# Splitting weights into high and low parts: the low parts move from VectorE to GpSimd in a kernel that schedules itself

## The chip, the cores and the metric

The kernel runs on one core of a Trainium2 chip. That core has a matrix engine (PE, with its weight loads shown apart as PEld), a vector engine (DVE), a scalar engine (ACT), GpSimd (POOL) and a queue engine that issues transfers (SP). The metric is the device time of one execution in microseconds; a kernel's figure is the median of its runs.

## The reference

```
sig = 1 / (1 + exp(-f_logit));  f = lb + (1 - lb) * sig          # (2, 6080, 256)
h[t] = f[t] * h[t-1] + (1 - f[t]) * x[t];  y[t] = h[t]           # scan along each sequence
a = relu(y.reshape(12160, 256) @ w_in)                           # w_in: 256 x 2048, float64
out = ((a * a) @ w_out).astype(float32)                          # w_out: 2048 x 256, float64
```

A gated scan over the tokens of two sequences, then a two-layer MLP with a squared ReLU. The weights arrive as float64, x and f_logit as float32.

## The kernel before

**Arithmetic.** PE multiplies in float32r, which keeps fewer bits than float32. So every operand v is split: `hi` is v rounded to float32r (made by ACT), `lo` is v - hi (made by DVE until now), and one product is three passes of PE: hi by hi, lo by hi and hi by lo. A few early products ("plain": `PLAIN_1`, `PLAIN_2`) use unsplit float32 operands, each costing PE four passes.

**Weights.** They come in as 64-bit integers and are turned into float32 on the chip, chunk by chunk, in `prepare_w`. For one chunk: DVE masks the exponent (`exponent`, L237), ACT rebiases it (`rebias`, L242), DVE sets sign and power (`power`, L270), DVE masks the mantissa, from a second copy loaded with a shift of some bytes (`mantissa_whole`, L257), or in two instructions (L248, L264), DVE multiplies both into the float32 weight (`whole`, L277), ACT rounds it to `w_h` (`high`, L292), and DVE subtracts to get `w_l` (`low`, L295). There are 15 chunks: two of 128 columns, three of 256, six of 512 and four of 1,024. The temporaries `e` and `w` are pools of two buffers, so a chunk's mantissa waits until the `high` and `low` of the chunk two before it have read theirs.

**Tokens.** The first 960 tokens are two blocks of 480 columns (`scan_x`): sigmoid (L352) and gate (L355) on ACT, a multiply (L361) and the scan (L368) on DVE, `high` (L384) on ACT, `low` on DVE: L388 for block 0, which also scales, and L393 for block 1, a plain subtraction. While these two blocks go through the MLP the weights are still being made. This stretch, up to the first product of pair 0 (the `bank_b` matmul), is called the ramp here. After it come 11 pairs of column blocks (up to 2 x 512), in a loop over 8 steps each, whose order is written out by hand and which the diff leaves alone.

**The scheduler.** In the ramp no order is written by hand. Each operation is a `Job` with an engine, a price in us and the jobs it comes after. `set_due` gives each a due time, counted back from the times at which PE is to need it (8.0 us plus 0.217 us for each pass). `emit_all` then plays the engines forward: at each step it takes the engine that can start soonest and, of the jobs ready there, the one due first. The order so found is the order in which each engine's instructions are written, so on the chip every engine runs them strictly in that order, each waiting for its inputs. Where the play leaves PE idle before 24 us, `idle` writes in matmuls on a dummy operand (`po<-t2h` in the trace) as filler.

The prices of the two engines concerned:

```python
def on_dve(n, emit, *after, rate=960):
    return Job("DVE", 0.075 + n / rate, emit, *after)

def on_act(n, emit, *after, base=0.1):
    return Job("ACT", base + n / 1200, emit, *after)
```

All transfers of the ramp are issued by SP. In the ramp's steady part POOL does nothing; its five instructions are memsets at the very start.

Of the kernel before, what the change touches and what calls it, by code (L numbers as in the profile page):

```python
# [7 lines left out]
F32 = mybir.dt.float32  # L8
# [8 lines left out]
ALU = mybir.AluOpType  # L17
# [6 lines left out]
def gated_scan_then_relu2_mlp(  # L24
# [13 lines left out]
    nc = tc.nc  # L38
# [18 lines left out]
    for row in range(T // seq):  # L57
        end = (row + 1) * seq
        while at < end:
            h = min(NB, (end - at) // 2)  # L60
# [32 lines left out]
    def pin(ins):  # L93
        return tc.keep_in_program_order(ins) if pinned[0] else ins


    class Job:

        def __init__(self, engine, cost, emit, *after, lag=None, load=0):
            self.engine, self.cost, self.emit, self.load = engine, cost, emit, load  # L100
            self.lag = cost + LAG[engine] if lag is None else lag
            self.after = [a for a in after if a is not None]
# [1 line left out]
            self.number = len(jobs)  # L104
            jobs.append(self)

    LAG = {"PE": 0.17, "DVE": 0.08, "ACT": 0.1, "SP": 0.0}
    SEEN = 0.04
    PASS = 0.217
    AWAIT = 0.02  # L110
# [15 lines left out]
    def on_dve(n, emit, *after, rate=960):  # L126
        return Job("DVE", 0.075 + n / rate, emit, *after)

    def on_act(n, emit, *after, base=0.1):
        return Job("ACT", base + n / 1200, emit, *after)  # L130

    def set_due():

        kids = {}
        for x in jobs:
            for y in x.after:
                kids.setdefault(id(y), []).append(x)
        done = set()

        def due(x):  # L140
            if x.number not in done:
                done.add(x.number)
                dues = [due(k) - SEEN for k in kids.get(id(x), [])] + ([x.due] if x.due else [])
                x.due = min(dues) - x.lag if dues else 1e9
            return x.due

        for x in reversed(jobs):
            due(x)

    def emit_all():  # L150

        free = {"PE": 1.2, "DVE": 1.2, "ACT": 2.0, "SP": 0.7}
        wire = 2.9
        left = {id(x): len(x.after) for x in jobs}
        kids = {}
        for x in jobs:
            for y in x.after:
                kids.setdefault(id(y), []).append(x)
        ready = {e: [] for e in LAG}

        def open_up(x):
            x.ready = max([y.end + SEEN for y in x.after] or [0.0])
            ready[x.engine].append(x)

        for x in jobs:
            if not x.after:
                open_up(x)
        while any(ready.values()):
            start, e = min(
                (max(free[e], min(x.ready for x in xs)), e) for e, xs in ready.items() if xs)  # L170
            x = min((x for x in ready[e] if x.ready <= start + AWAIT),
                    key=lambda x: x.number if e == "SP" else x.due)
            start = max(start, x.ready)
            if e == "PE":
                idle(start - free[e], start)
            ready[e].remove(x)
            pinned[0] = True
            x.emit()
            pinned[0] = False
            free[e] = start + x.cost  # L180
            x.end = start + x.lag
            if x.load:
                wire = max(start + 2.2, wire)
                wire = x.end = wire + x.load / (265e3 if wire < 6.3 else 375e3)
            for k in kids.get(id(x), []):
                left[id(k)] -= 1
                if not left[id(k)]:
                    open_up(k)
        assert all(x.end is not None for x in jobs)
# [32 lines left out]
    def prepare_w(m, a, n, load):  # L222
# [3 lines left out]
        hi, lo = w_h2[m // 2][:, a:a + n], w_l2[m // 2][:, a:a + n]  # L226
        tmp = {}
# [64 lines left out]
            pin(nc.scalar.activation(out=hi, in_=tmp["w"], func=AF.Copy))  # L292

        def low():
            pin(nc.vector.tensor_tensor(out=lo, in0=tmp["w"], in1=hi.bitcast(F32), op=ALU.subtract))  # L295

        old = sets[-2] if len(sets) > 1 else (None,) * 8
        e = on_dve(n, exponent, load, old[4], rate=1920)
# [11 lines left out]
        w = on_dve(n, whole, *f, s)  # L310
# [3 lines left out]
                k: on_act(P, lambda k=k: scaled(k), w, base=0.25)  # L314
                for k in range(b // P, min(b + n, D) // P)})
        h = on_act(n, high, w)
        l = on_dve(n, low, h)
        sets.append((e, i, f, s, w, h, l))
        raw_jobs.setdefault(m // 2, []).extend((e, s) if m in SHIFT else (e, *f, i, s))
        return h, l  # L320
# [7 lines left out]
    def operand(name, part):  # L328
        return xs.tile([P, NB], F32R, tag=f"{name}{part}", name=f"{name}{part}")
# [3 lines left out]
    def scan_x(j):  # L333

        t, n, first = blocks[j]
        f, x, g = {}, {}, {}

        def fetch(got, src, nm, k):
            def emit():
                if not got:  # L340
                    sb = fx.tile([P, KD, NB], F32, tag=f"{nm}{j}", name=f"{nm}in")
                    got.update({i: sb[:, i, :n] for i in range(KD)})
                    got["all"] = sb
                at = slice(k, k + 1)
                pin(nc.sync.dma_start(out=got["all"][:, at, :n], in_=src[:, at, t:t + n]))
            return emit

        def sig(k):
            if j == 0 and k == 0:
                o = io.tile([P, KD, NB], F32, tag="ob", name="gate")  # L350
                g.update({i: o[:, i, :n] for i in range(KD)})
            pin(nc.scalar.activation(out=f[k], in_=f[k], func=AF.Sigmoid))  # L352

        def lin(k):
            pin(nc.scalar.activation(  # L355
                out=g[k] if j == 0 else f[k], in_=f[k], func=AF.Identity,
                scale=olb_sb[:, k:k + 1], bias=lb_sb[:, k:k + 1],
            ))

        def mul(k):  # L360
            pin(nc.vector.scalar_tensor_tensor(  # L361
                out=x[k], in0=f[k], scalar=1.0, in1=x[k], op0=ALU.subtract, op1=ALU.mult,
            ))

        def run(k):
            i = n_scan[0] // KD % 2
            n_scan[0] += 1
            pin(nc.vector.tensor_tensor_scan(  # L368
                out=x[k], data0=g[k] if j == 0 else f[k], data1=x[k],
                initial=0.0 if first else st[k][1 - i], op0=ALU.mult, op1=ALU.subtract,  # L370
            ))
            x_in[j] = x

        def keep(k):

            scale = {"func": AF.Identity, "scale": olb_sb[:, k:k + 1]} if j == 0 else {"func": AF.Copy}
            pin(nc.scalar.activation(out=st[k][j], in_=x[k][:, n - 1:n], **scale))

        def high(k):
            if j not in x_h:  # L380
                x_h[j] = [operand(o, "h")[:, :n] for o in HOME[j]]
                x_l[j] = [operand(o, "l")[:, :n] for o in HOME[j]]
            scale = {"func": AF.Identity, "scale": olb_sb[:, k:k + 1]} if j == 0 else {"func": AF.Copy}
            pin(nc.scalar.activation(out=x_h[j][k], in_=x[k], **scale))  # L384

        def low(k):
            if j == 0:
                pin(nc.vector.scalar_tensor_tensor(  # L388
                    out=x_l[j][k], in0=x[k], scalar=olb_sb[:, k:k + 1],
                    in1=x_h[j][k].bitcast(F32), op0=ALU.mult, op1=ALU.subtract,  # L390
                ))
            else:
                pin(nc.vector.tensor_tensor(  # L393
                    out=x_l[j][k], in0=x[k], in1=x_h[j][k].bitcast(F32), op=ALU.subtract))

        def loads_of(ks):
            return {(nm, k): Job("SP", 0.45, fetch(got, src, nm, k),
                                 load=P * 4 * n)
                    for k in ks for nm, got, src in (("f", f, fT), ("x", x, xT))}

        def jobs_of(loads, kept):
            out = {}
            for k in range(KD):
                a = on_act(n, lambda k=k: sig(k), loads.get(("f", k), loads["f", 0]))
                if j == 0:
                    c = on_dve(n, lambda k=k: mul(k), a, loads.get(("x", k), loads["x", 0]))
                    b = on_act(n, lambda k=k: lin(k), a, base=0.27)
                else:
                    b = on_act(n, lambda k=k: lin(k), a, base=0.27)
                    c = on_dve(n, lambda k=k: mul(k), b, loads.get(("x", k), loads["x", 0]))  # L410
                d = on_dve(n, lambda k=k: run(k), c, b, kept[k], rate=480)
                h = on_act(n, lambda k=k: high(k), d, base=0.27 if j == 0 else 0.1)
                s = on_act(1, lambda k=k: keep(k), d)
                l = on_dve(n, lambda k=k: low(k), h)
                out[k] = h, l, s, d
            return out

        return loads_of, jobs_of
# [390 lines left out]
    for js, m in tiles:  # L809
        while pend and pend[0][0] < m - 2:  # L810
            second_job(*pend.pop(0))
        high, low = first_jobs(js, m)
# [10 lines left out]
    after = [x for y in x_jobs for k in range(KD) for x in y[k][:3]] + [in_of[6][0][0]]  # L823
# [13 lines left out]
    sig, lin, neg, run, sub, hi, lo = pair_steps(0)  # L837
# [26 lines left out]
    first, high, low = sums_w(0)  # L864
# [108 lines left out]
    for p, (_, h, _) in enumerate(pairs):  # L973
# [4 lines left out]
        for s in range(STEPS):  # L978
# [62 lines left out]
            if closing:  # L1041
                n = len(groups)
# [21 lines left out]
    n = len(groups)  # L1064
# [5 lines left out]
    at, h, _ = pairs[p]  # L1070
# [52 lines left out]
```

## Time and profile before

| | us |
|---|---|
| median of 3 runs (lowest to highest) | 997.66 (997.41 to 998.53) |
| the profiled execution, its own time | 996.66 |
| its span, first to last instruction | 994.7 |
| PE busy in the span | 989.3 |
| DVE busy | 748.7 |
| ACT busy | 721.6 |
| POOL busy | 0.7 |

The granted clock of TensorE is 1.00 over the whole execution. A matmul's duration in the trace is longer than the step to the next one, because matmuls overlap: it is the step, the difference of two starts, that says what one costs.

### The profile page before, as it was taken

The page shows a single profiled execution, that of the slowest core. Times are in us where ns is not written, and L with a number is a line of the kernel's source. Part 1 is how long each engine was busy: PE and PEld are TensorE (multiplying, and loading weights), DVE is VectorE, ACT ScalarE, POOL GpSimd, SP SyncE. Part 2 cuts the span into 40 slices and gives each one's busy share as a digit, 9 for nine tenths or more (in the row PEclk, how much of TensorE's full clock was granted, in tenths as well). Part 3 has the DMA queues.
Part 4 walks back from the last instruction along what each step waited for, and adds up shares of the span by engine and source line. Part 5 has one row for each costly group of instructions (what it writes and reads, how often), then busy time and mean ns, then how long its engine had stood idle before and what let it go on. Part 6 is the DMA issues. An engine that isn't in the chain of part 4 may idle for free.

```text
span 994.7 us, 11306 instructions
## 1 busy us (share of the span) xinstructions
PE 989.3 (99%) x4357; PEld 818.2 (82%) x4357; DVE 748.7 (75%) x929; ACT 721.6 (73%) x981; POOL 0.7 (0%) x5
## 2 busy tenths in 40 slices
PE   9999999999999999999999999999999999999998
PEld 5888888888888888888888888888888888888887
DVE  8997888687678677778767867867776876786555
ACT  8997988767677677776776767667677677676664
POOL 0000000000000000000000000000000000000000
PEclk9999999999999999999999999999999999999999
DMA  8942102102100200210210110021021021000001
GB/s 286 344 168 85 41 1 85 43 0 64 64 1 22 78 29 20 65 43 1 65 64 1 53 71 4 22 64 43 0 85 43 1 60 63 1 1 21 22 1 40
DMA packets 15893, 53.80 MB, mean 54 GB/s; under 512 B 1888, under 2 KB 4192, under 8 KB 15328
## 3 DMA queue, kind: packets, MB, share of 16 engines
q1 hardware_dynamic: 15552, 52.84, 15.4%
q8 instruction: 34, 0.56, 0.2%
q10 hardware_dynamic: 288, 0.25, 0.1%
q14 instruction: 19, 0.16, 0.1%
HBM read 40.63 MB, written 12.45 MB: 53 GB/s over the span
## 4 chain that ended last, share of the span: by engine, by line
PE 94%; DVE 3%; ACT 2%; DMA 1%; issue 0%; SPq 0%
PE po L434 68%; PE bank_b L434 24%; PE ph L434 2%; DMA shifted<-in_w_dram 1%; DMA fin<-in_f_logit_dram 0%; DVE e L270 0%; DVE gl L740 0%; DVE w_l L295 0%; DVE w L277 0%; DVE e L237 0%; DVE w L257 0%; DVE xin L368 0%; ACT e L242 0%; ACT w_h L292 0%; ACT fin L512 0%
## 5 line engine op out<-in xcount | busy, mean ns | idle before, releaser
L964 DVE TENSOR_TENSOR gl<-r,gh 128x1024 fp32r<-128x1024 f32 (+1 forms) x174 | 212.3, 1220 | 146.2 <-ACT r L933 89.7
L434 PE MATMUL po<-gh,w_h 128*128 128x512 f32 (+1 forms) x764 | 296.8, 388 | 0.0
L434 PE MATMUL po<-gh,w_l 128*128 128x512 f32 (+1 forms) x764 | 296.7, 388 | 0.0
L434 PE MATMUL po<-gl,w_h 128*128 128x512 f32 (+1 forms) x764 | 296.3, 388 | 0.0
L1037 ACT ACTIVATE r<-r 128x1024 f32<-128x1024 f32 (+1 forms) x87 | 92.1, 1058 | 131.5 <-DVE r L1031 131.5
L434 PEld LDWEIGHTS po<-gh,w_h 128*128 128x128 f32 x764 | 143.5, 188 | 30.8 <-ACT gh L730 0.6
L434 PEld LDWEIGHTS po<-gl,w_h 128*128 128x128 f32 x764 | 143.4, 188 | 29.1 <-DVE gl L964 0.5
L434 PEld LDWEIGHTS po<-gh,w_l 128*128 128x128 f32 x764 | 143.5, 188 | 28.1 <-issue 0.4
L942 ACT ACTIVATE gh<-r 128x1024 fp32r<-128x1024 f32 (+1 forms) x81 | 85.6, 1057 | 34.5 <-DVE r L937 34.5
L1031 DVE TENSOR_TENSOR r<-po,u 128x512 f32<-128x512 f32 (+1 forms) x88 | 60.6, 688 | 62.4 <-PE po L434 61.6
L1002 ACT ACTIVATE c<-bank_b 128x512 f32<-128x512 f32 (+1 forms) x88 | 52.5, 597 | 70.9 <-PE bank_b L434 70.9
L933 ACT ACTIVATE r<-r 128x1024 f32<-128x1024 f32 (+1 forms) x93 | 98.3, 1057 | 2.9
L929 ACT ACTIVATE gh<-r 128x1024 fp32r<-128x1024 f32 (+1 forms) x93 | 98.4, 1058 | 2.8
L937 DVE SCALAR_TENSOR_TENSOR r<-r 128x1024 f32<-128x1024 f32 (+1 forms) x81 | 98.2, 1213 | 0.0
L1024 DVE TENSOR_TENSOR r<-po,c 128x512 f32<-128x512 f32 (+1 forms) x88 | 60.6, 688 | 5.6 <-PE po L434 1.1
L1033 DVE TENSOR_TENSOR r<-bank_b,p 128x512 f32<-128x512 f32 (+1 forms) x88 | 60.6, 689 | 0.0
L1023 ACT ACTIVATE u<-bank_b 128x512 f32<-128x512 f32 (+1 forms) x88 | 52.5, 596 | 11.1 <-PE bank_b L434 1.9
L1017 ACT ACTIVATE p<-po 128x512 f32<-128x512 f32 (+1 forms) x88 | 50.8, 577 | 0.8 <-PE po L434 0.8
L1058 ACT ACTIVATE r<-bank_b 128x512 f32<-128x512 f32 (+1 forms) x87 | 50.2, 578 | 0.0
L532 DVE TENSOR_TENSOR_SCAN xin<-fin,small,xin 128x1024 f32<-128x1024 f32 (+1 forms) x20 | 46.6, 2331 | 0.0
L434 PE MATMUL po<-t1h,w_h 128*128 128x512 f32 (+1 forms) x88 | 34.3, 389 | 0.0
L434 PE MATMUL po<-t1h,w_l 128*128 128x512 f32 (+1 forms) x88 | 34.2, 389 | 0.0
(166 smaller groups left out, 1558.3 us busy)
## 6 DMA issues: line engine op xcount, KB each, us to landing
fin<-in_f_logit_dram SPq DMA_DIRECT2D x20, 512.0 KB, 4.2
xin<-in_x_dram SPq DMA_DIRECT2D x20, 512.0 KB, 3.6
out_dram<-ob SPq DMA_DIRECT2D x20, 512.0 KB, 2.6
shifted<-in_w_dram SPq DMA_DIRECT2D x14, 511.5 KB, 5.4
raw<-in_w_dram SPq DMA_DIRECT2D x4, 1024.0 KB, 6.9
raw<-in_w_dram SPq DMA_DIRECT2D x6, 512.0 KB, 5.9
out_dram<-ob SPq DMA_DIRECT2D x7, 240.0 KB, 2.0
fin<-in_f_logit_dram SPq DMA_DIRECT2D x4, 240.0 KB, 4.6
```

What stands on the lines that cost most here:

```text
L434: pin(nc.tensor.matmul(*args, **kw))
L929: pin(nc.scalar.activation(out=self.gh[:, :, :self.h], in_=self.r, func=AF.Square))
L933: pin(nc.scalar.activation(out=self.r, in_=self.r, func=AF.Square))
L937: pin(nc.vector.scalar_tensor_tensor(out=self.r, in0=self.r, scalar=0.0, in1=self.r, op0=ALU.max, op1=ALU.mult))
L942: pin(nc.scalar.activation(out=self.gh[:, :, :self.h], in_=self.r, func=AF.Copy))
L964: pin(nc.vector.tensor_tensor(out=self.gl[:, :, :self.h], in0=self.r, in1=self.gh[:, :, :self.h].bitcast(F32), op=ALU.subtract))
L1002: pin(nc.scalar.activation(out=c1, in_=B[:, :h], func=AF.Copy))
L1023: pin(nc.scalar.activation(out=u2, in_=B[:, :h], func=AF.Copy))
L1024: pin(nc.vector.tensor_tensor(out=r0[:, 0, :h], in0=Dk[:, :h], in1=c1, op=ALU.add))
L1031: pin(nc.vector.tensor_tensor(out=r0[:, 1, :h], in0=A[:, :h], in1=u2, op=ALU.add))
L1033: pin(nc.vector.tensor_tensor(out=r1[:, 1, :h], in0=B[:, :h], in1=p5, op=ALU.add))
L1037: pin(nc.scalar.activation(out=r0[:, :, :h], in_=r0[:, :, :h], func=AF.Relu))
```

## The change

The scheduler gets a fifth engine, POOL, with a price of 0.15 us plus one us for 460 columns, a lag of 0.15 us and a first free time of 2.0 us. Two kinds of jobs go there: `low` of all 15 weight chunks, and `low` of block 1's tokens (two instructions, one for each half of the model dimension). `low` of block 0, and the pairs' own `lo`, stay on DVE. Because prices and engine change, the scheduler may also find another order for every other instruction of the ramp.

```diff
-    LAG = {"PE": 0.17, "DVE": 0.08, "ACT": 0.1, "SP": 0.0}
+    LAG = {"PE": 0.17, "DVE": 0.08, "ACT": 0.1, "POOL": 0.15, "SP": 0.0}
...
+    def on_pool(n, emit, *after):
+        return Job("POOL", 0.15 + n / 460, emit, *after)
+
...
-        free = {"PE": 1.2, "DVE": 1.2, "ACT": 2.0, "SP": 0.7}
+        free = {"PE": 1.2, "DVE": 1.2, "ACT": 2.0, "POOL": 2.0, "SP": 0.7}
...
         def low():
-            pin(nc.vector.tensor_tensor(out=lo, in0=tmp["w"], in1=hi.bitcast(F32), op=ALU.subtract))
+            pin(nc.gpsimd.tensor_tensor(out=lo, in0=tmp["w"], in1=hi.bitcast(F32), op=ALU.subtract))
...
         h = on_act(n, high, w)
-        l = on_dve(n, low, h)
+        l = on_pool(n, low, h)
...
             else:
-                pin(nc.vector.tensor_tensor(
+                pin(nc.gpsimd.tensor_tensor(
                     out=x_l[j][k], in0=x[k], in1=x_h[j][k].bitcast(F32), op=ALU.subtract))
...
-                l = on_dve(n, lambda k=k: low(k), h)
+                l = (on_pool if j else on_dve)(n, lambda k=k: low(k), h)
```

## Rows read from the trace of the kernel before

**Rows 1.** The page's first part: busy us, share of the span, instructions of each engine.
```profile
PE 989.3 (99%) x4357; PEld 818.2 (82%) x4357; DVE 748.7 (75%) x929; ACT 721.6 (73%) x981; POOL 0.7 (0%) x5
```
**Rows 2.** Busy time by stretch; PE, PEld, DVE, ACT, POOL, clock, DMA share, GB/s.
```profile
9.05:20.15 11.10, 10.83 (x28) 4.80 (x27) 10.70 (x25) 11.10 (x26) 0.00 (x0) 1.00 0.79 297
20.15:90.70 70.55, 70.41 (x321) 59.59 (x320) 65.70 (x95) 65.14 (x99) 0.00 (x0) 1.00 0.65 232
...
5.00:59.40 54.40, 53.99 (x222) 40.79 (x221) 52.20 (x91) 53.12 (x94) 0.00 (x0) 1.00 0.88 323
```
**Rows 3.** Timeline of PE: start, us, instruction; start, one wait, end of the ramp.
```profile
1.31 7.90 PE L434 MATMUL po<-t2h 128*128 128x480 f32 x26 [1.31 <-POOL t2h L473]
9.05 3.38 PE L434 MATMUL ph<-xin,t4l 128*128 128x480 f32 x8
...
58.86 0.38 PE L434 MATMUL po<-gl,w_h 128*128 128x480 f32 x1
59.38 0.49 PE L434 MATMUL ph<-b11h,w_h 128*128 128x480 f32 x1
...
90.49 0.38 PE L434 MATMUL po<-gl,w_h 128*128 128x480 f32 x1
90.71 0.39 PE L434 MATMUL bank_b<-b11h,w_h 128*128 128x512 f32 x1
```
**Rows 4.** The start's gate and scan: timelines of ACT and DVE.
```profile
6.38 0.77 ACT L355 ACTIVATE gate<-fin,small 128x480 f32<-128x480 f32 x1
...
7.41 1.15 DVE L368 TENSOR_TENSOR_SCAN xin<-gate,xin 128x480 f32<-128x480 f32 x1
```
**Rows 5.** Chain of waits within the ramp: start, us, what; its stretches on DVE and DMA.
```profile
10.78 0.66 DVE xin L361
...
29.84 0.69 DVE e L270
...
37.58 7.30 DMA shifted<-in_w_dram
...
58.37 0.96 ACT w_h L292
```
**Rows 6.** Busy time of line 295 alone, by stretch: length, DVE busy, clock, DMA share.
```profile
5.00:20.00 15.00, 1.53 (x5) 1.00 0.84 307
20.00:30.00 10.00, 1.66 (x3) 1.00 0.92 321
30.00:45.00 15.00, 2.74 (x4) 1.00 0.90 332
45.00:59.00 14.00, 1.23 (x1) 1.00 0.89 334
59.00:73.00 14.00, 3.60 (x3) 1.00 0.31 108
```
**Rows 7.** DVE's groups by line and form in the first 100 us: two of those moved.
```profile
L295 DVE TENSOR_TENSOR w_l<-w,w_h 128x1024 fp32r<-128x1024 f32 x4 | 4.9, 1220 | 0.1
...
L393 DVE TENSOR_TENSOR b22l<-xin,b22h 128x480 fp32r<-128x480 f32 x1 | 0.7, 653 | 0.0
```
**Rows 8.** DVE's timeline around 31 us: one-input and two-input instructions, back to back.
```profile
30.44 0.42 DVE L257 TENSOR_SCALAR w<-shifted 128x512 int32<-128x512 int32 x1
30.77 0.42 DVE L237 TENSOR_SCALAR e<-raw 128x512 int16<-128x512 int16 x1
31.11 0.69 DVE L295 TENSOR_TENSOR w_l<-w,w_h 128x512 fp32r<-128x512 f32 x1
31.71 0.69 DVE L277 SCALAR_TENSOR_TENSOR w<-w,e 128x512 f32<-128x512 int32 x1
```
**Rows 9.** POOL's groups: its only instruction on a wide tile.
```profile
L473 POOL MEMSET t2h<- 128x512 f32 x1 | 0.5, 525 | 0.3 <-POOLq L1112 0.3
```
**Rows 10.** Timelines where PE needs a low part soonest: ACT's high, DVE's low, PE.
```profile
23.03 0.63 ACT L292 ACTIVATE w_h<-w 128x512 fp32r<-128x512 f32 x1
...
24.05 0.69 DVE L295 TENSOR_TENSOR w_l<-w,w_h 128x512 fp32r<-128x512 f32 x1
...
25.01 0.38 PE L434 MATMUL ph<-b11h,w_l 128*128 128x480 f32 x1
```
**Rows 11.** Waits of PE's weight loads, whole span: us, times, longest.
```profile
PEld ph L434 <- ACT w_h L292: 0.5, 1, 0.5
...
PEld ph L434 <- DVE w_l L295: 0.3, 2, 0.2
```
**Rows 12.** Waits of ACT from 59 to 91 us: us, times, longest.
```profile
ACT r L727 <- PE ph L434: 3.6, 6, 0.9
```

## The prediction, made before the changed kernel was run

> **What bounds the kernel now.** I read the page's busy times first: PE is busy for 989.3 of 994.7 us, DVE and ACT for about three quarters, POOL for 0.7 [rows 1]. A busy PE need not be a PE at work, so the second look is at the steps between matmuls. From 90.49 to 90.71 us it is 0.22 us, a 480-column pass, and so on through the ramp. The only work that the change can touch lies before the first product of pair 0 at 90.71 us [rows 3]; all that follows is written out by hand and runs at PE's pace. So the question is how early PE gets through the ramp.
>
> The third look is at busy time by stretch. From PE's first real matmul at 9.05 us to 90.70 PE is idle for 0.27 us (11.10 less 10.83) and then for 0.14 (70.55 less 70.41) [rows 2]; one wait, before 59.38 us, makes 0.3 of it (0.52 from start to start, less a step of 0.22) [rows 3]. At most 0.5 us can be won there, the one filler pass in this stretch included. The fourth look is at the chain of waits within the ramp. It goes along DVE without a break worth naming from 10.78 us to about 37, then through a transfer of shifted weight words (7.30 us) and ACT to the wait at 59.38 [rows 5]. DVE has 2.2 us of idle time between 5.0 and 59.4 us (54.40 less 52.20) [rows 2]. So DVE is nearly full there, and PE has hardly any wait that a lighter DVE could take away. The kernel stands on an edge: DVE time given back is worth next to nothing, DVE time lost comes out at PE.
>
> **The change part by part.** *What DVE gives up.* Until 59 us line 295 is busy for 1.53 + 1.66 + 2.74 + 1.23 = 7.2 us in 12 instructions [rows 6], and the two token instructions for 2 x 0.65 = 1.3 [rows 7]. A DVE instruction of 0.69 us lets the next one start after 0.60 [rows 8], so the 14 give back about 8.5 less 14 x 0.09, or 7.2 us. After 59 us three chunks of 1,024 columns, 3.6 us busy [rows 6], give back 3.4.
>
> *What POOL takes on.* Until 59.4 us: 2 x 128 + 3 x 256 + 6 x 512 + 1 x 1,024 + 2 x 480 = 6,080 columns in 14 instructions. By the diff's own price this is 6,080 / 460 + 14 x 0.15 = 15.3 us, and 2.4 us for one of 1,024 columns, which takes DVE 1.22 [rows 7]. No row shows POOL reading anything. The nearest is its memset, 525 ns for 512 columns [rows 9]: one stream at 1.03 ns a column. If a subtraction cost no more than one stream, the 14 would take 6.2 us; if its two reads and one write went one after the other at that rate, 18.7 + 2.1 = 20.8. I take 15.3, which lies between, nearer the upper end, as two inputs are nearer three streams than one. The Trainium skill, GPSIMD Engine Reference, section 3.1, gives 4,497 ns for such an instruction on 2,048 columns; by that the sum would be 6,080 x 2.2 ns = 13.4 us, an estimate, and the forecast two microseconds lower.
>
> *Whether the two engines run side by side.* This decides. A one-input DVE instruction takes 512 columns in 0.33 us from start to start, a two-input one in 0.60 [rows 8]. DVE thus reads about the same amount per time in both, two operands at half the pace or one at the full pace, as if both its ways of reading were taken in either case. Nearly all DVE work of the ramp is of these two kinds: I read from it that a POOL instruction with two operands would have to read in DVE's place. That is a reading, as no row has POOL and DVE at work together. The ends are: no effect on each other, and strict turns, every POOL microsecond lost to DVE. I take turns. The Trainium skill, SBUF — State Buffer, section Who interferes with whom, says that a two-input DVE instruction and a GpSimd instruction that reads shut each other out for a whole instruction; no run here shows that yet.
>
> *The sum.* With turns DVE loses 15.3 us, has 7.2 back and 2.2 idle: it is 5.9 us behind at 59.4. A POOL instruction that starts in a DVE wait, or under the last 0.09 us of a DVE instruction, takes less, so I put PE's delay at 4.5 (an estimate). Bounds: nothing at a price of 6.2, and 20.8 - 7.2 - 2.2 = 11.4 us at the highest. After 59.4 us POOL's three chunks (7.1 us by the diff's price) against 3.4 given back cost DVE 3.7; it has 31.3 us there with an ACT that waits for PE for 3.6 us [rows 12], so work is ahead of PE, and I add nothing. If that cover were gone it would be up to 3.7 more.
>
> *The new waits.* Until now a chunk's mantissa needed nothing from another engine to find the buffer `w` free but ACT's rounding, since `low` was an earlier DVE instruction. Now it waits for POOL. Behind it on DVE stand the squares' low parts, which PE reads, and the scans; a late mantissa also holds back the next shifted load, which took 7.30 us on the chain [rows 5]. And a low part itself comes later: after the rounding of the 512-column chunk at 23.03 + 0.63 = 23.66 us, DVE was done at 24.74 and PE read at 25.01 [rows 10]. POOL by its price is done at about 24.95. That is just in time only if nothing is in its way; here PE's wait begins. PE's weight loads wait for a low part for 0.3 us today, and 0.5 for a high one [rows 11]. *The start.* The gate is done at 6.38 + 0.77 = 7.15 us, the scan starts at 7.41 [rows 4], and PE's first real matmul is at 9.05 [rows 3]; with the scan's 1.15 the earliest is 8.3 to 8.4, so 0.7 us is all that a better order could win. The other edits (prices, lag, first free time) cost no instruction. No transfer is added or moved to another queue.
>
> **The rivals.** *Side by side* (0.37). POOL runs next to DVE at the diff's price. For it: the 1.22 us that a moved instruction takes on DVE fit twice into what POOL has, and the scheduler counts POOL in. The wait at 59.38 goes (0.3), perhaps a little at the start; the time is 997.4, between 996.6 and 998.6. This is the rival on the other side; it decides if DVE's two-input instructions keep their 0.69 us while POOL is busy. *POOL is the one that is kept out* (0.11). DVE runs back to back and POOL gets in only when DVE waits. DVE then keeps its pace, and PE stops at its weight loads for `w_l` until DVE stands still too. The deficit is the same 5.9 us, and up to 3.7 of the late chunks come on top: 1003 to 1007. *POOL slower than its price, next to an undisturbed DVE* (0.04). A chunk of 1,024 at three streams would take 3.3 us for 2.4: PE waits up to 0.9 us, once and not per chunk, since the feeding engines go on meanwhile: 998.6. *Well faster* (0.03): by over 2 us cannot come from 0.5 us of idle PE and 0.7 of start; it would need something that I don't see.
>
> **How the numbers follow.** The sum stands against the profiled execution, 996.66 us with a span of 994.7: 996.66 + 4.5 = 1001.2. The median of the runs is 1.0 above that, so the forecast is 1002.2 us. Turns with DVE behind gets 0.45. Its own range is 999 to 1007. The range over all cases is 996.9 to 1007.0: it takes in most of side by side, and leaves out 0.1 below and 0.1 above, with the upper bound of POOL's price. 0.2%, or 2 us, is about what can be told from no change. Slower by more: 0.45 less 0.02 for a small effect, and 0.11, so 0.54. Within: 0.37, 0.04 and 0.02, so 0.43. Faster: 0.03.
>
> **What would show it.** POOL's subtractions of 1,024 columns at 2.4 us or more. DVE instructions with two inputs above their 0.69 and 1.22 us wherever POOL is busy, or POOL ones far above price in the second rival. New waits of PE's weight loads for `w_l`, of DVE for POOL, and PE's first `bank_b` matmul at about 95 us in place of 90.71. From there on, the same steps as before. I am wrong if DVE's durations don't move, or if that matmul stands within 1 us of 90.71.

## The result, and the profile after

| | before | after |
|---|---|---|
| median, us (lowest to highest, runs) | 997.81 (997.41 to 998.53, 4) | 1010.36 (1009.67 to 1011.30, 4) |
| ratio, 95% interval | | 1.0122 (1.011 to 1.0135) |
| profiled execution: own time, span | 996.66, 994.7 | 1009.78, 1008.0 |

The change makes the kernel 12.55 us slower. The forecast had the sign (slower, 1002.2) and not the size: the time lies above its range, which ended at 1007.0. Line numbers after are three higher than before from L132 on: L298 is the old L295, L396 the old L393, L437 PE's L434.

The page's first part of the kernel after, to set beside [rows 1]:

```profile
PE 993.6 (99%) x4358; PEld 819.8 (81%) x4358; DVE 751.9 (75%) x912; ACT 722.2 (72%) x981; POOL 31.0 (3%) x22
```

DVE has 17 instructions fewer and is yet busy for longer. PE's share is 99% as before, so the share doesn't tell where the time went. The places do. PE's timeline of the kernel after; these rows answer to those at 59.38 and 90.71 us in [rows 3]:

```profile
65.17 0.38 PE L437 MATMUL ph<-b11h,w_h 128*128 128x480 f32 x1
65.39 0.38 PE L437 MATMUL po<-gh,w_h 128*128 128x480 f32 x1
70.99 0.77 PE L437 MATMUL ph<-b11h,w_l 128*128 128x480 f32 x1 [5.22 <-POOL w_l L298]
71.56 0.60 PE L437 MATMUL ph<-b11l,w_h 128*128 128x480 f32 x1
71.96 0.60 PE L437 MATMUL ph<-b21h,w_h 128*128 128x480 f32 x1
...
75.08 0.38 PE L437 MATMUL ph<-t1h,w_l 128*128 128x480 f32 x1
...
103.68 0.39 PE L437 MATMUL bank_b<-b11h,w_h 128*128 128x512 f32 x1
```

The first product of pair 0 stands at 103.68 instead of 90.71 us: 12.97 later, which is the whole loss. Read off these rows, it comes in three pieces. The group that began at 59.38 begins at 65.17: 5.8 us. Counted matmul by matmul, PE is that late (6.0 us) already at 35.81, after waits for DVE and ACT of which the longest is 1.37 us, at 18.52. One wait for a low part from POOL, 65.39 to 70.99 less a step of 0.22: 5.4 us. Then ten steps take 4.09 us (70.99 to 75.08), where ten at 0.22 take 2.2: 1.9. Sum 13.1.

The third piece is the clock. Busy time by stretch of the kernel after (columns as in [rows 2]):

```profile
64.00:66.00 2.00, 1.77 (x9) 1.19 (x7) 2.00 (x4) 2.00 (x5) 1.91 (x1) 1.00 0.90 248
66.00:68.00 2.00, 0.00 (x0) 0.00 (x0) 2.00 (x3) 2.00 (x3) 2.00 (x1) 1.00 0.95 366
68.00:70.00 2.00, 0.00 (x0) 0.00 (x0) 0.74 (x1) 1.68 (x2) 2.00 (x1) 0.54 0.10 41
72.00:74.00 2.00, 2.00 (x7) 1.65 (x6) 2.00 (x3) 0.60 (x2) 0.00 (x0) 0.50 0.00 0
74.00:76.00 2.00, 2.00 (x9) 1.71 (x8) 2.00 (x3) 0.77 (x2) 0.00 (x0) 0.76 0.00 0
```

PE does nothing from 66 to 70 us. The granted clock falls from 1.00 to 0.54 in that time, stays at 0.50 (1.2 of 2.4 GHz) while PE works again, and comes back between 74 and 76. The steps of 0.40 us are the same instructions at the lower level. So a stop of 5.4 us stands for 7.3 us in these rows.

POOL's timeline of the kernel after:

```profile
24.33 1.30 POOL L298 TENSOR_TENSOR w_l<-t2h,w_h 128x512 fp32r<-128x512 f32 x1 [2.22 <-ACT w_h L295]
...
35.60 1.31 POOL L298 TENSOR_TENSOR w_l<-w,w_h 128x512 fp32r<-128x512 f32 x1 [1.29 <-ACT w_h L295]
...
47.22 1.55 POOL L298 TENSOR_TENSOR w_l<-w,w_h 128x512 fp32r<-128x512 f32 x1 [5.01 <-ACT w_h L295]
51.02 2.56 POOL L298 TENSOR_TENSOR w_l<-w,w_h 128x1024 fp32r<-128x1024 f32 x1 [2.26 <-ACT w_h L295]
64.09 6.85 POOL L298 TENSOR_TENSOR w_l<-w,w_h 128x1024 fp32r<-128x1024 f32 x1 [10.51 <-ACT w_h L295]
77.32 2.41 POOL L298 TENSOR_TENSOR w_l<-w,w_h 128x1024 fp32r<-128x1024 f32 x1 [6.38 <-ACT w_h L295]
```

At best an instruction takes about the scheduler's price (512 columns 1.30 us for 1.26, 1,024 columns 2.41 for 2.38); four of the six with 512 columns take 1.48 to 1.61. The one at 64.09 takes 6.85. DVE's timeline shows what happens to the other side:

```profile
35.68 1.51 DVE L260 TENSOR_SCALAR w<-shifted 128x512 int32<-128x512 int32 x1
...
47.65 2.20 DVE L280 SCALAR_TENSOR_TENSOR w<-w,e 128x1024 f32<-128x1024 int32 x1
...
64.11 1.22 DVE L526 SCALAR_TENSOR_TENSOR xin<-fin,xin 128x1024 f32<-128x1024 f32 x1
65.25 0.68 DVE L547 TENSOR_TENSOR fin<-xin 128x512 f32<-128x512 f32 x1
65.85 1.15 DVE L743 TENSOR_TENSOR gl<-r,gh 128x960 fp32r<-128x960 f32 x1
66.92 0.69 DVE L240 TENSOR_SCALAR e<-raw 128x1024 int16<-128x1024 int16 x1
67.52 1.22 DVE L273 SCALAR_TENSOR_TENSOR e<-raw,e 128x1024 int16<-128x1024 int16 x1
70.97 0.43 DVE L260 TENSOR_SCALAR w<-shifted 128x512 int32<-128x512 int32 x1 [2.23 <-POOL w_l L298]
```

The first two rows are DVE held up: 0.42 us of work takes 1.51, and 1.22 takes 2.20. Each ends after POOL does: POOL is done at 36.91 (35.60 + 1.31) and 48.77 (47.22 + 1.55), DVE 0.28 and 1.08 us later. The other six are the opposite. DVE runs five instructions back to back at their usual durations while POOL stands; 68.74 us is the end of the fifth, and 2.20 us later, about a POOL subtraction's own length, POOL is done. DVE's next mantissa waits for exactly that instruction. So in this ramp either engine is kept waiting by the other.

### The profile page after: what moved, and what is told of

Read it like the earlier page. It is cut to its first block, busy times and chain, and to the rows that moved or that the text cites. A ratio compares the mean times of both kernels' runs of the same rounds, so it can differ in the third digit from the quotient of the medians.

```text
span 1008.0 us, 11326 instructions
## 1 busy us (share of the span) xinstructions
PE 993.6 (99%) x4358; PEld 819.8 (81%) x4358; DVE 751.9 (75%) x912; ACT 722.2 (72%) x981; POOL 31.0 (3%) x22
## 4 chain that ended last, share of the span: by engine, by line
PE 93%; DVE 3%; ACT 2%; DMA 1%; POOL 1%; issue 1%; SPq 0%; DVEq 0%
PE po L437 67%; PE bank_b L437 24%; PE ph L437 2%; POOL w_l L298 1%; DVE e L273 1%; DMA shifted<-in_w_dram 1%; DVE w L280 0%; DVE gl L743 0%; DMA raw<-in_w_dram 0%; ACT w_h L295 0%; ACT gh L733 0%; DVE w L260 0%; DVE e L240 0%; ACT e L245 0%; DVE xin L371 0%
## 5 line engine op out<-in xcount | busy, mean ns | idle before, releaser
L437 PE MATMUL po<-gl,w_h 128*128 128x512 f32 (+1 forms) x764 | 296.8, 388 | 0.7 <-DVE gl L743 0.7
L437 PE MATMUL po<-gh,w_h 128*128 128x512 f32 (+1 forms) x764 | 296.4, 388 | 0.0
L437 PE MATMUL po<-gh,w_l 128*128 128x512 f32 (+1 forms) x764 | 296.2, 388 | 0.0
L437 PEld LDWEIGHTS po<-gl,w_h 128*128 128x128 f32 x764 | 143.4, 188 | 30.9 <-DVE gl L743 1.3
L437 PEld LDWEIGHTS po<-gh,w_h 128*128 128x128 f32 x764 | 143.4, 188 | 30.1 <-ACT ob L907 0.5
L437 PEld LDWEIGHTS po<-gh,w_l 128*128 128x128 f32 x764 | 143.6, 188 | 28.2 <-POOL w_l L298 0.2
L437 PE MATMUL po<-b21l,w_h 128*128 128x512 f32 (+1 forms) x88 | 34.2, 389 | 0.0
L437 PE MATMUL po<-t1l,w_h 128*128 128x512 f32 (+1 forms) x88 | 34.2, 389 | 0.0
```

The costliest lines, as they stand in the source:

```text
L437: pin(nc.tensor.matmul(*args, **kw))
```

## The experiments

Each "+" is the difference of the medians of a run and of the kernel before in the same comparison.

**Order or engine.** The change moves instructions and, through the prices, reorders all others. Two kernels separate them: the order of after with all 17 subtractions back on DVE, and the order of before with all 17 on POOL.

```diff
 # e2, against the kernel after, in both low()
-pin(nc.gpsimd.tensor_tensor(
+pin(nc.vector.tensor_tensor(
 # f1, against the kernel before, in both low()
-pin(nc.vector.tensor_tensor(
+pin(nc.gpsimd.tensor_tensor(
```

> The changed kernel with its plan unchanged (POOL still counted as an engine when the order is found), but all 17 subtractions are issued on DVE at their places. Theory (what costs is POOL reading beside DVE): DVE has 10.7 us of work that the plan does not count, yet no POOL in its way: 998 to 1001 us. Rival (the new order of the instructions is what costs): 1006 to 1010 us.

> The kernel before with its plan (the scheduler still prices the 17 subtractions as DVE's), but they are issued on POOL. With the run that has the new plan and all on DVE (1002.0, 4.4 us above before) this makes a table of two by two. Theory (the new order costs 4.4 us and POOL's reading beside DVE the other 8 of 12.6, each by itself): 1004 to 1007 us. Rival (the two only cost together, since a plan without POOL's work has room for it): 998 to 1001 us.

The order alone: 1002.00 us, 1.0045 (1.003 to 1.006), +4.4, first `bank_b` at 96.10; this lies between the two expectations and misses both. The engine alone: 1004.66 us, 1.0069 (1.0052 to 1.0086), +7.1, at 97.95, as its theory had it. Together they make 11.5 of the 12.5; the rest is within the intervals. DVE's timeline of the kernel with the new order on DVE shows what the order does:

```profile
15.47 0.66 DVE L396 TENSOR_TENSOR b22l<-xin,b22h 128x480 fp32r<-128x480 f32 x1
...
16.58 0.42 DVE L280 SCALAR_TENSOR_TENSOR t4h<-w,e 128x256 f32<-128x256 f32 x1
...
17.12 0.66 DVE L396 TENSOR_TENSOR t1l<-xin,t1h 128x480 fp32r<-128x480 f32 x1
```

Before, the same two subtractions stood at 20.21 and 23.48, behind weights that PE uses sooner; `t4h` was at 15.45. The scheduler gives POOL a job as soon as it is ready, because POOL is idle, and fills the time it believes DVE has won. When these instructions take DVE's time after all, PE loses: it is busy for 68.38 us between 20.15 and 90.70, 70.41 before [rows 2]. PE's timeline of the same kernel:

```profile
62.40 0.38 PE L437 MATMUL ph<-b11h,w_h 128*128 128x480 f32 x1
...
75.61 0.48 PE L437 MATMUL ph<-b22h,w_h 128*128 128x480 f32 x1 [0.66 <-ACT r L730]
...
85.58 0.48 PE L437 MATMUL ph<-b11h,w_h 128*128 128x480 f32 x1 [0.58 <-ACT r L730]
```

The group of 59.38 us is 3.0 late, and `bank_b` 5.4: nearly half of the order's cost comes after that group. Which of the moved jobs cost it was not tried apart.

What the engine alone does is on PE's timeline of the kernel with the old order on POOL, and in the window that answers to 5.00:59.40 in [rows 2]:

```profile
28.67 0.48 PE L434 MATMUL ph<-b11h,w_l 128*128 128x480 f32 x1 [0.73 <-POOL w_l L295]
...
37.34 0.48 PE L434 MATMUL ph<-b11h,w_l 128*128 128x480 f32 x1 [1.47 <-POOL w_l L295]
...
55.44 0.49 PE L434 MATMUL ph<-b11h,w_l 128*128 128x480 f32 x1 [0.72 <-POOL w_l L295]
...
68.38 0.49 PE L434 MATMUL ph<-b11h,w_l 128*128 128x480 f32 x1 [0.96 <-POOL w_l L295]
```
```profile
5.00:65.50 60.50, 55.95 (x221) 41.32 (x221) 53.85 (x77) 53.47 (x93) 19.29 (x15) 1.00 0.80 293
```

The group of 59.38 us starts at 65.52, 6.1 late. The first three waits, from start to start less a step, make 3.4 of it: they are waits for POOL's low part itself. Of the 6.1 us by which the stretch is longer, DVE is busy for 1.7 (53.85 less 52.20) and idle for the other 4.4. Ten DVE instructions in it are longer than the same ones before, by 0.3 to 1.1 us each and 8.0 together; DVE is rid of 7.2 us there.

**Reading or writing.** The kernel before, with POOL doing extra work that nobody waits for: reads of `w_h`, or a copy of one column and then memsets.

```diff
 # e3, in high(), pieces of up to 512 columns
...
+    pin(nc.gpsimd.tensor_tensor(out=idle_out[:, :min(WN, n)], in0=x, in1=x, op=ALU.subtract))
 # e4, in high()
+    pin(nc.gpsimd.tensor_copy(idle_out[:, :1], hi[:, :1].bitcast(F32)))
+    for o in range(0, 2 * n, min(WN, n)):
+        pin(nc.gpsimd.memset(idle_out[:, :min(WN, n)], 0.0))
```

> The kernel before, with a POOL subtraction of the same columns beside it after each rounding of a weight chunk (w_h minus w_h into a scratch tile that nobody reads, in pieces of at most 512 columns). No engine waits for POOL, DVE keeps its own subtractions. Theory (turns): DVE's instructions are held while POOL reads, and PE's first product of pair 0 is later by 3 to 11 us: 1001 to 1009 us. Rival (side by side): 997 to 999 us.

> The kernel before, with POOL memsets at the same places (after a copy of one column, two memsets of each chunk's columns, some 17 us of POOL that write and do not read). Theory (it is the reading that DVE and POOL take in turns): DVE's durations stay, 997 to 999 us. Rival (any POOL access to the memory holds DVE): the one-input DVE instructions at least are held, 1000 us or more.

Reads: 1005.57 us, 1.0085 (1.007 to 1.01), +7.9. Writes: 997.79, 1.0002 (0.9993 to 1.0012). Both theories came as written. So it is POOL's reading, and not its being busy or the scheduling, that DVE pays for. POOL's timeline of the kernel with reads already has an instruction far above price (1.3 us for 512 columns); in the one with memsets, a copy of a single column, which is a read too, stood for 8.27 us:

```profile
64.94 14.97 POOL L297 TENSOR_TENSOR idle_out<-w_h 128x512 f32<-128x512 f32 x1 [9.38 <-ACT w_h L294]
```
```profile
16.93 8.27 POOL L295 COPY idle_out<-w_h 128x1 f32<-128x1 f32 x1 [3.10 <-ACT w_h L294]
```

**The two engines alone.** A kernel of its own, POOL subtractions of 1,024 columns beside rows of one kind of DVE instruction each.

```python
go(); read()                       # POOL: back = a - b, released by a short DVE instruction
for o in range(12): two(o, a)      # DVE: outs[o] = a - b; further rows: chained, one input,
                                   # PSUM operand, POOL memsets in place of read(), waits for ACT
```

> A kernel of its own that leaves out the whole computation: POOL subtracts 1,024 columns once beside rows of DVE instructions of one kind. Theory (DVE with two inputs, or one input at double pace, and a reading POOL take turns; POOL is kept out while DVE runs without a gap): alone POOL takes 2.4 us; beside 12 two-input instructions with no wait among them it takes up to 12 x 1.14 + 2.4 = 16 us and DVE keeps 1.22; where each waits for the one before, POOL gets in after one of them (under 4.8 us) and one DVE instruction takes some 2.4 us longer; beside one operand from the accumulation memory, and beside POOL memsets, neither changes. Rival (a fair exchange of turns): POOL gets in after at most one DVE instruction in every row.

DVE's timeline of that kernel (groups of equal instructions in one row, the duration being that of the group): two inputs beside a POOL read, one input beside it, a PSUM operand beside it, two inputs beside POOL memsets, then both kinds without POOL. Below it, POOL's row beside the first.

```profile
9.99 15.86 DVE L61 TENSOR_TENSOR o<-a,b 128x1024 f32<-128x1024 f32 x12
...
43.47 11.87 DVE L81 TENSOR_SCALAR o<-a 128x1024 f32<-128x1024 f32 x16
...
55.70 9.66 DVE L86 TENSOR_TENSOR o<-bank,a 128x512 f32<-128x512 f32 x16
...
65.73 13.72 DVE L61 TENSOR_TENSOR o<-a,b 128x1024 f32<-128x1024 f32 x12
...
96.79 4.63 DVE L61 TENSOR_TENSOR o<-a,b 128x1024 f32<-128x1024 f32 x4
101.34 2.49 DVE L109 TENSOR_SCALAR o<-a 128x1024 f32<-128x1024 f32 x4
```
```profile
10.03 3.38 POOL L58 TENSOR_TENSOR back<-a,b 128x1024 f32<-128x1024 f32 x1 [0.34 <-DVE a L54]
```

Twelve two-input instructions take 13.72 us beside POOL's writes and 15.86 beside one POOL read: 2.1 lost for a subtraction that takes 2.38 alone. The one-input kind loses about as much (11.87, against 9.7 for 16 at the 0.6 us a step of the last row). With one operand in PSUM DVE loses nothing (9.66 is 16 steps of 0.60), and POOL is done in 2.35. One part of the expectation failed: beside twelve instructions without a wait POOL was to be kept out for up to 16 us, and it was done in 3.38; in no row did it take longer, which is what the rival said. What the rows do show is the turn that the forecast assumed, and on this point the Trainium skill (SBUF — State Buffer, Who interferes with whom) agrees: DVE with two SBUF inputs contends with a GpSimd instruction that reads, not with one that only writes. By the same page of the Trainium skill (section Summary: rules for kernel authors) the one that issues second is blocked until the first finishes. The 14.97 us above are more than that, POOL standing through DVE instructions that were issued long after it; here the measurement decides.

**The long wait.** Three edits at chunk 10, whose low part took the 6.85 us: make it on DVE, or start it later (two delays).

```diff
 # e1, against the kernel after, in low()
+eng = nc.vector if m == 10 else nc.gpsimd
...
 # h1 (WN // 2 columns of memset) and h2 (2 * WN), ahead of chunk 10's subtraction
+pin(nc.scalar.activation(out=lo[:, :1], in_=hi[:, :1].bitcast(F32), func=AF.Copy))
+pin(nc.gpsimd.memset(lo[:, :WN // 2].bitcast(F32), 0.0))
```

> The changed kernel with its plan unchanged, but one of the 17 moved instructions, the low part of chunk 10 and 11, goes back to DVE. Theory (turns, and one instruction kept out): the 5.4 us wait and the 1.8 us at the lower clock after it go, the 5.8 us lost before stay: 1003 us, 0.995 of the changed kernel or less. Rival (the low parts are late because POOL is slow, DVE is not held): one instruction of 17 gains at most the 1.2 us by which POOL is slower: 1009 us.

> The changed kernel, its order unchanged; only before the low part of chunk 10 and 11 ACT copies one column of it and POOL then sets 256 columns of it, so that POOL's subtraction starts some 0.6 us later. Theory (whether POOL is kept out hangs on the moment at which it starts): it may get in after one DVE instruction; then the 5.4 us wait and the lower clock go, as with that part on DVE: 1005 to 1008 us. Rival (this row of DVE instructions keeps POOL out at any start): 1010 to 1011 us.

> The same with 1,024 columns set first, so that POOL's subtraction starts some 1.3 us later. Theory (the moment): let in, 1005 to 1008 us, in at least one of the two kernels. Rival (this row of DVE instructions keeps POOL out at any start): 1010 to 1012 us in both.

On DVE: 1007.97 us, 1.0105 (1.009 to 1.012), +10.3, which misses both expectations. The long stop and the lower clock are gone, 7.3 us by the rows above, and only 2.2 come back. Windows of that kernel say why:

```profile
54.00:65.50 11.50, 11.50 (x54) 9.93 (x53) 11.04 (x13) 11.50 (x16) 0.00 (x0) 1.00 0.65 237
65.50:91.00 25.50, 21.83 (x97) 17.50 (x95) 25.40 (x29) 19.36 (x29) 5.64 (x2) 1.00 0.19 61
```

From 65.5 us on DVE has 0.1 us of idle time in 25.5, and PE 3.7. Part of DVE's busy time is again turns, on its timeline (the scan takes 2.34 elsewhere and the other 0.69; POOL's next two chunks hold them):

```profile
74.21 4.50 DVE L536 TENSOR_TENSOR_SCAN xin<-fin,small,xin 128x1024 f32<-128x1024 f32 x1
...
82.84 2.89 DVE L548 TENSOR_TENSOR fin<-xin 128x512 f32<-128x512 f32 x1
```

ACT waits for just these two (2.7 and 1.6 us), and PE for ACT behind each (1.67 us at 80.40, 1.09 at 86.97). So the stop for POOL hides a lateness of DVE that comes out anyway. That only 2.2 of the 7.3 us come back holds for this kernel, in which DVE also has the 1.1 us of the subtraction to do again. The two later starts gave 1010.62 us each, 1.0134 (1.0117 to 1.0151) and 1.0133 (1.0118 to 1.0148). The subtraction, now at 65.41 and 66.20, took 6.24 and 5.59 and again ended only after DVE had come to a wait. For these three starts the moment makes no difference, as the rivals said.

**The scheduler's model.** After, with the scheduler told that a POOL job takes DVE's time as well; and after, with only block 1's token subtractions back on DVE, price and engine.

```diff
 # f2, in emit_all
+if e == "POOL":
+    free["DVE"] = max(free["DVE"], start) + x.cost
 # g2, in scan_x
-l = (on_pool if j else on_dve)(n, lambda k=k: low(k), h)
+l = on_dve(n, lambda k=k: low(k), h)
```

> The changed kernel with one line more in the scheduler: while it plays a POOL job, DVE's next free time is put off by the job's price, so the order is found for two engines that take turns. Theory (turns): the order fits again and the instruction kept out for 6.8 us goes, but DVE still has 22 us of POOL in its way for 10.7 given back: 1002 to 1007 us, under the changed kernel and over the one before. Rival (the scheduler's order hardly matters): 1009 to 1011 us.

> The changed kernel without its two token subtractions on POOL: they are DVE jobs again, for the scheduler too; the 15 weight chunks stay on POOL. Theory (POOL has no due order and does the tokens at once, at 14.8 us, where they hold DVE by 2 us on the way to the weights that PE waits for at 18.5 us): PE is ahead by 1 to 2 us at 28 us, and the time is 1008 to 1010 us, or lower if nothing is kept out. Rival (the tokens are free on POOL and cost 1.1 us on DVE): 1010 to 1012 us.

A plan that counts the turns: 1004.83 us, 1.0077 (1.0062 to 1.0092), +7.3. That is what the old order with POOL gives, and 5.2 better than after: this plan wins back the part that the order costs, and not the turns. Tokens back on DVE: 1008.01, 1.0105 (1.0087 to 1.0123), +10.4. The gain is not the one that was expected, PE getting its first operands sooner: PE reached the first weight group 1.9 us later (30.09 for 28.19), since now a 256-column subtraction was kept out: begun at 17.51, it took 6.66 us. What did go is the long stop: chunk 10's subtraction took 2.68 us, and PE's longest wait after 59 us was 2.08, at 71.83.

**The late chunks.** Before, with only chunks 12 to 15 on POOL.

```diff
+eng = nc.gpsimd if m >= 12 else nc.vector
```

> The kernel before with its plan, only the low parts of the last two chunks (12 to 15) on POOL. It tries the step of the prediction that adds nothing after 59 us. Theory of that step (work there is ahead of PE): 997 to 999 us. Rival (DVE is the bound there too): 1000 us or more.

997.36 us, 1.0001 (0.9991 to 1.001), first `bank_b` at 91.16, as the theory had it: where DVE has room, the move is free, and still wins nothing. These are two of the three chunks after 59 us; the first of them, chunk 10, is not in this test.

**What lets POOL in.** Three more kernels of their own ran the same POOL subtraction beside longer rows: four kinds of rows with three starts, three kinds with twelve starts, and rows of 12 and 11 two-input instructions with zero, one or two POOL reads in between while DVE waits for them. The last in its core, shortened:

```python
def stretch(n):
    wait = back * one         # DVE, 64 columns; waits for POOL's last read
    wait = copy(wait)         # ACT: releases POOL
    back = wait - b           # POOL, 1,024 columns
    for o in range(n): two(o % 7)
for n in (12, 11):
    for alone in (0, 1, 2):
        for _ in range(6):
            stretch(n)
            for _ in range(alone): stretch(0)
```

> A kernel of its own that leaves out the whole computation: POOL subtracts 1,024 columns once in each of twelve stretches, beside two rounds of DVE instructions in one of four mixes (the ramp's own mix of one- and two-input instructions with 16- and 32-bit strided reads; plain two-input; 16-bit strided two-input; one-input and two-input in turn), started 0.3, 0.6 or 0.9 us after DVE. Theory (whether POOL is kept out hangs on the kind of DVE instruction that follows): in the ramp's mix or the strided ones POOL takes 5 us or more in all three starts, in plain two-input under 4.8 us. Rival (it hangs on the moment): in each mix some starts are short and some long. Second rival (POOL always gets in at the next change of DVE's instruction): under 4.8 us in all twelve.

> A kernel of its own that leaves out the whole computation: as the mixed streams, with twelve starts each, some 0.07 us apart, beside plain two-input instructions of 1,024 columns, 16-bit strided two-input ones, and the ramp's mix. Theory (the moment decides whether POOL gets in at the next change of DVE's instruction or is kept out until DVE stops): in the plain stream and the ramp's mix both kinds occur, durations lie near 2.3 to 3.6 us or near 12 to 16 us and nothing between. Rival (a steady rule by the kind of instruction): one kind only in each stream. For the strided stream both say only short ones, as before.

> Not the reference: a kernel of its own that times DVE and POOL beside each other and writes part of the output. Rows of 12, then of 11, two-input DVE subtractions of 1,024 columns without waits (with the one that releases POOL, 13 or 12 DVE instructions a row), and one POOL subtraction of 1,024 columns ready at each row's start. Each sort six times with nothing between the rows, six times with one POOL subtraction between them while DVE waits, and six times with two. It let POOL in and kept it out by turns in the run before this one. Theory memory (a subtraction that got in over a busy DVE is kept out the next time, and one that met a waiting DVE clears that): with nothing between, 2.4 to 3.5 us and 14 to 15.5 us alternate, for 12 and for 11 alike; with one or two between, all at 2.4 to 3.5 us. Theory count (what decides is whether the number of DVE instructions since is odd or even): rows of 11 with nothing between are all alike, in or out, and one and two between behave differently from each other. Theory moment (it hangs on the exact offset of the two starts): no such regularity in any of the six sorts.

The first gave 2.4 to 3.0 us three times beside the row of 16-bit strided instructions and, beside each of the other three rows, both that and 12 to 15.5: the theory of the kind missed, and the rival (each mix both ways) too, by the strided row. The second showed the pattern: with starts moved in twelve steps, two-input rows gave 2.96, 15.39, 2.83, 15.26 and so on in strict turn, the ramp's mixture 2.50, 12.20, 2.37, 12.06; and rows of the 16-bit instruction L270, each waiting for the one before it, let POOL in all twelve times. POOL's timeline of the third kernel; nothing between the rows, then one read between them (every second line):

```profile
9.97 2.96 POOL L100 TENSOR_TENSOR back<-wait,b 128x1024 f32<-128x1024 f32 x1 [9.53 <-ACT wait L99]
25.86 15.46 POOL L100 TENSOR_TENSOR back<-wait,b 128x1024 f32<-128x1024 f32 x1 [12.94 <-ACT wait L99]
41.94 2.96 POOL L100 TENSOR_TENSOR back<-wait,b 128x1024 f32<-128x1024 f32 x1 [0.63 <-ACT wait L99]
57.84 15.45 POOL L100 TENSOR_TENSOR back<-wait,b 128x1024 f32<-128x1024 f32 x1 [12.94 <-ACT wait L99]
...
105.91 2.96 POOL L100 TENSOR_TENSOR back<-wait,b 128x1024 f32<-128x1024 f32 x1 [0.63 <-ACT wait L99]
121.81 2.34 POOL L100 TENSOR_TENSOR back<-wait,b 128x1024 f32<-128x1024 f32 x1 [12.94 <-ACT wait L99]
124.77 2.97 POOL L100 TENSOR_TENSOR back<-wait,b 128x1024 f32<-128x1024 f32 x1 [0.63 <-ACT wait L99]
```

In turn with nothing between (11 instead of 12: 2.96 and 14.32), always in with one or two between, for 12 and for 11. Count and moment are out for such rows; the expectation of memory came as written. Whether POOL's read between or DVE's wait for it clears the state, these rows can't tell, as they come together.

To carry it over to the kernel: after, with one small read on POOL behind chunk 8's.

```diff
+if m == 8:
+    x = hi[:, :64].bitcast(F32)
+    pin(nc.gpsimd.tensor_tensor(out=idle_out, in0=x, in1=x, op=ALU.subtract))
```

> The changed kernel, and right after the subtraction of chunk 8's low part on POOL (51.02 us) one more of 64 columns, w_h - w_h, into a buffer of its own that nobody reads. Its price is not given to the scheduler, so every other instruction stands where it stood. Theory memory (a subtraction that got in over a busy DVE leaves the next one out, unless POOL reads once beside a waiting DVE in between): the small one is kept out until DVE next waits (54.9 us), and then the subtraction of 1,024 columns at 64.1 us, which took 6.85 us, is let in: 2.4 to 3.5 us. DVE's L260 waits for POOL no more, PE's wait at 65.39 us shrinks below 1.5 us from 5.4 and the clock keeps its upper level there; the total then is that of the run with this chunk on DVE or a little less, 1005.5 to 1009. Theory place (what keeps it out is the row of DVE instructions behind it, whatever POOL did before): it takes 5.5 to 7 us again, and the time is 1009.5 to 1011.

1011.49 us, 1.0132 (1.0115 to 1.0149). POOL's timeline:

```profile
54.56 0.48 POOL L303 TENSOR_TENSOR idle_out<-w_h 128x64 f32<-128x64 f32 x1
65.17 6.85 POOL L300 TENSOR_TENSOR w_l<-w,w_h 128x1024 fp32r<-128x1024 f32 x1 [10.12 <-ACT w_h L297]
```

The theory of memory missed; that of place has its 6.85 us, and its time (1009.5 to 1011) misses by 0.5. The small read did not find DVE waiting; it got in between two DVE instructions, so it was no clean test. But the memory of the streams cannot be the whole rule in this ramp either: after, eight POOL subtractions from 14.76 to 35.60 us all got in and held a DVE instruction up by 0.5 to 1.1 us, with none kept out between them. What decides there stays open.

## Why the prediction was wrong, step by step

- **What bounds the kernel** held in its first half: PE had nothing to win, and each kernel in which POOL read beside DVE in the ramp's first 59 us was slower. That DVE's lost time is what comes out at PE held only in part, see the sum.
- **What POOL takes on** held: 2.41 us for 1,024 columns (2.4 forecast), 1.30 for 512 (1.26). The Trainium skill's figure (GPSIMD Engine Reference, section 3.1), 2.25 by half of its 2,048 columns, an estimate, is 0.16 below that.
- **Whether the two engines run side by side** held: turns, shown by reads (+7.9) against writes (nothing) and by the two engines alone (2.1 us lost to one read). But not every POOL microsecond was one of DVE's: under the old order DVE's instructions were held up by 8.0 us until PE's group of 59.38, not 15.3. *Side by side*, at 0.37, is out.
- **The sum** failed in its size and in its path, even for the engine alone. Under the old order, which is what it reckoned with, moving the 17 to POOL costs 7.1 us, 4.5 forecast. PE's group of 59.38 us came 6.1 late there, and 1.0 came after it; the discount from 5.9 to 4.5 had no row under it. That 5.9 is so near 6.1 is luck: DVE's busy time grew by 1.7 us, and the larger part of PE's loss is waits for POOL's low parts, a path that is named under the new waits and has no term in the sum.
- **The step that failed** is the sentence that the other edits (prices, lag, first free time) cost no instruction. They cost none, and they reorder all: with the same instructions on the same engine, the new order costs 4.4 us. The text before the prediction says that the scheduler may find another order; the sum has no term for it, which puts it at nothing. It can be read off the diff that the new prices free DVE of 17 jobs in the plan; if turns are forecast, the plan is wrong by just those, and its order is one for a machine that isn't there. With this term and the engine's as it was measured, 4.4 + 7.1, the sum would have been 1009. The order's 4.4 alone, on top of the forecast, gives 1006.6: the missing term and the engine's too small one are both needed to reach what was measured.
- **After 59.4 I add nothing** held under the old order for chunks 12 to 15 (997.36), and missed by 1.0 us for chunk 10, whose low part PE waits for at 68.38. It failed under the new one: with chunk 10 back on DVE, DVE has no idle time left from 65.5 to 91 and turns show at PE, and the order alone already costs 2.4 us after that group. The cover was named, and that the new order would use it up was not asked.
- **POOL is the one that is kept out** was made a rival of the turns. Both happen in one ramp: turns at 35.60 and 47.22 us, POOL kept out at 64.09; under the old order as well, where the subtraction of 512 columns at 34.16 took 3.13 us. That rival's range, 1003 to 1007, lies too low as well. Its stop of PE and the fall of the clock (7.3 us by the rows) stand largely in place of a lateness that was there anyway: 2.2 us came back when the stop went. That PE's clock falls in such a stop, 1.9 us, was not forecast.
- **The new waits** were of the kinds named: PE for `w_l`, and DVE's mantissa for POOL (2.23 us at 70.97). PE's first for `w_l` came at the matmul named (25.01 before) under the old order, at 28.67; under the new one the only long one is that before 70.99.

## What to carry to other kernels

When a scheduler of the kernel's own is told of another engine, forecast two things apart: the instructions that move, and the order that the new prices make; the second is measured by keeping the new order and putting the work back. An engine that is idle is not free if a full one is held up by its reads: a POOL subtraction that met a busy DVE held it up by up to 1.1 us for 512 columns and 2.2 for 1,024, nearly twice the 0.60 and 1.14 that DVE takes for it. Where a low part is due soon, POOL may stand through a whole unbroken row of DVE instructions, as it did for 6.85 us here; and a stop of PE can cost more than itself, as the 5.4 us here did by the lower clock after it.

## What the runs showed of the hardware that was not expected

- A waiting POOL instruction can be passed by many later DVE instructions (15.46 us for a subtraction of 2.34, twelve two-input instructions in a row); in the ramp even a copy of one column stood for 8.27 us. Beside rows of two-input instructions without a wait, let in and kept out alternate strictly, and one round in which DVE waits for POOL's read resets it. The ramp does not follow this rule as it stands.
- DVE instructions with one operand in PSUM, and POOL's memsets, cost the other engine nothing (9.66 us for 16, 13.72 for 12).
